# Wider vector operations, a stepped product and one PSUM pool in a fused SSM-convolution and GLU kernel

## The chip, the cores and the metric

The kernel runs on one core of a Trainium2 chip. The metric is the device time of one execution in microseconds. Before the change it is 245.11 us (median of 3 runs, 244.93 to 247.17). The engines of the core are PE (matrix products; PEld is its weight load), DVE (vector), ACT (scalar), POOL and SP, which issues most of the transfers.

## The reference

S = 2048 positions, D = 640 channels, F = 1728; everything is bfloat16.

```python
xn = layernorm(A_q)                                  # over the 640 channels
# A: a short shift filter, a product, and a long convolution over the sequence
k_shift[s] = sum over m of k[s - m] * shift_k[:, m]  # 4 taps
kv = k_shift * v
y = irfft(rfft(kv, 2*S) * rfft(ssm_k, 2*S))[:S]      # long convolution
y = xn * (y + kv * ssm_D)
# B: gated linear unit
h = sigmoid(xn @ w_gate) * (xn @ w_up)
out = A_q + y + h @ w_down
```

## The kernel before, in words

**The GLU.** The sequence is cut into four stretches `tr` of 512 positions. For each, `rec_norm` normalises and `rec_tp` transposes (on PE for 0 and 1, by a transfer through DRAM for 2 and 3), and `rec_fc` makes 14 blocks `fc` of 128 hidden channels: gate and up, five matmuls of 128x512 each (L761), into PSUM tiles of the kind `g` (one bank). ACT takes the sigmoid (L726) and DVE multiplies (L729, L732), with an eviction `ev_u` for the up half where it is in `UP`. `rec_down` makes, for each of the 16 rows `m` of 128 positions, two halves of 320 channels with 14 matmuls each (L775), each half in a `g` bank of its own and added to `acc` by DVE (`fin`, L781). `store` writes `acc` out.

**The convolution.** The FFT is written as matrix products. The channels lie as 4 groups of 160 on the partitions; they are worked off in two halves of five sub-blocks each, `idx` 0 to 9. Each sub-block has 16 channels per group, as two lots `b` of `JS` = 8: channel j and channel j+40. Its steps:
- `rec_kv` (DVE): four multiplications of k with a tap (L474, L475) and three additions (L479), 1024 elements per partition each, and the product with v (L492), which reads both its inputs with a step and writes `kvt` densely. The temporaries lie in `ta`, `tb` and `kvt`.
- `rec_st1` (PE, L512, 32-row blocks), evicted into T; `rec_st2` (PE, L532, 64-row blocks), evicted into S.
- `rec_prod` (DVE): the complex product. Q = X times the other half of H, in the tile P (one buffer, `P2`); X = X times H (L564); then the difference (L568) and the sum (L570) of the two partition halves. Each is done for `b` = 0 and 1 apart, 1024 wide. For the sub-blocks in `SWAP` (3 to 9) two transfers on SP's queue (L551) first bring H's other half into P, and Q is one 128-partition operation for each `b` (L555); for 0 to 2 Q takes two 64-partition operations for each `b` (L561).
- `rec_st3` (PE, L583), evicted into V (in VX).

After the last sub-block `rec_st4` makes six units `u` of up to three rows (L614), evicts them (`ev_y`), multiplies by xn (L621) and adds to `acc` (L622).

**The order.** Every instruction group is recorded by `plan.op`, which numbers it. `ORDER` lists all numbers in the order in which they are emitted, and each engine and each queue runs its own in that order. Most evictions, and the norms of the later rows, can run on ACT or DVE: those whose number is in `ON_DVE` run on DVE. Stores go to ACT's queue, or to SP's if listed.

**The buffers.** `emit` gives each tile a buffer of its kind from `SLOTS`. In PSUM there are three `c` tiles of two banks and two `g` tiles of one bank, apart from each other. `load_h` (L448) brings the convolution filter in with 8 transfers for each part, and `hD` (L452) adds D to its first element, with a step. `load_shift` spreads the taps with two matmuls (csh, L395).

Of the kernel before, what the change touches and what calls it, by code (L numbers as in the profile page):

```python
# [42 lines left out]
def _dft_tables():  # L43
# [82 lines left out]
]  # L126
ON_DVE = [
    52, 106, 108, 110, 142, 148, 150, 506, 514, 534, 562, 574, 646, 831, 883, 917, 922, 970, 971, 972, 973, 975, 976,
    978, 979, 981, 982, 983, 984, 990, 993, 994, 998, 999
# [7 lines left out]
class _Plan:  # L137
# [54 lines left out]
    def emit(self, order, make):  # L192
# [4 lines left out]
        occupant["VB"][0] = "early"  # L197
        where = {}
        for n, o in enumerate(order):
            assert o.deps - {o.seq} <= done  # L200
            mine = []
            for b, tag in o.alloc:
                if b in where:
                    continue
                free = [i for i, c in enumerate(occupant[tag]) if (c is None or left[c] == 0) and (tag, i) not in mine]
                i = min(free, key=lambda i: (occupant[tag][i] is not None, last.get(occupant[tag][i], 0), i))
                mine.append((tag, i))
                occupant[tag][i] = b
# [12 lines left out]
def kernel(  # L221
# [65 lines left out]

    xnd = dr.tile([NQ * P, DM], BF16, name="xnd")
# [3 lines left out]
             "ta": 1, "tb": 1, "T": 2, "S": 2, "P2": 1, "VA": 1, "VB": 1, "c": 3, "g": 2}  # L292
# [3 lines left out]
        "ht0": ([P, 16, 2, N2], BF16), "ht1": ([P, 24, 2, N2], BF16), "kvt": ([P, 2, N2, JS], BF16),  # L296
        "ta": ([P, N2, 2, JS], BF16), "tb": ([P, N2, 2, JS], BF16), "T": ([P, 2 * K1, 2, JS, G], BF16), "S": ([P, 2, 2, JS, G * K1], BF16),
        "P2": ([P, 2, JS, G * K1], BF16),
        "c": ([P, 2, 512], F32), "g": ([P, 512], F32),
# [5 lines left out]
    def make(b, tag, i):  # L305
# [8 lines left out]
        if tag == "VB":  # L314
            return V2[:, 1]
        shape, dt = SHAPE[tag]
        if b.startswith("pst"):
            shape, dt = [P, NC, P], BF16
# [5 lines left out]
        pool = ps if tag in ("c", "g") else wk  # L324
        return pool.tile(shape, dt, name=f"{tag}{i}", tag=f"{tag}{i}")
# [24 lines left out]

    SWAP = (3, 4, 5, 6, 7, 8, 9)
    UP = {(tr, fc) for tr in range(1, 4) for fc in range(12)}
    ZC = (0, 1, 2, 3, 4, 5, 6, 7, 8, 9)
    KT = (0, 1, 2, 3, 4, 5, 6, 7, 8, 9)
    TD = 1
    ACT_STAT = (1, 3)
# [546 lines left out]
```

## Time and profile before

| | before |
|---|---|
| median of 3 runs | 245.11 us |
| profiled execution | 245.07 us |
| its span, first to last instruction | 243.3 us |
| PE busy | 234.2 us (96%), 3700 matmuls |
| PEld busy | 139.4 us (57%) |
| DVE busy | 199.1 us (82%), 335 instructions |
| ACT busy | 186.2 us (77%), 277 instructions |
| granted TensorE clock | 1.0 throughout |

Busy times are of the profiled execution. An operation's mean is its own length; DVE's operations can overlap by some 0.1 us, so means times counts come to more than the busy time. PE's matmuls are pipelined and their ends are modelled, so the time between the starts of two matmuls says more than the length of one.

### The profile page before, as it was taken

The page shows a single profiled execution, that of the slowest core. Times are in us where ns is not written, and L with a number is a line of the kernel's source. Part 1 is how long each engine was busy: PE and PEld are TensorE (multiplying, and loading weights), DVE is VectorE, ACT ScalarE, POOL GpSimd, SP SyncE. Part 2 cuts the span into 40 slices and gives each one's busy share as a digit, 9 for nine tenths or more (in the row PEclk, how much of TensorE's full clock was granted, in tenths as well). Part 3 has the DMA queues.
Part 4 walks back from the last instruction along what each step waited for, and adds up shares of the span by engine and source line. Part 5 has one row for each costly group of instructions (what it writes and reads, how often), then busy time and mean ns, then how long its engine had stood idle before and what let it go on. Part 6 is the DMA issues. An engine that isn't in the chain of part 4 may idle for free.

```text
span 243.3 us, 8435 instructions
## 1 busy us (share of the span) xinstructions
PE 234.2 (96%) x3700; PEld 139.4 (57%) x3700; DVE 199.1 (82%) x335; ACT 186.2 (77%) x277; POOL 0.7 (0%) x6
## 2 busy tenths in 40 slices
PE   8899999999999999999989999998999999999994
PEld 2645445775446546666645555566776565456762
DVE  3623436499899999999999999999989994898973
ACT  5566756978999999796889999986887787656510
POOL 1000000000000000000000000000000000000000
PEclk9999999999999999999999999999999999999999
DMA  6999999998999595199949498593432286972383
GB/s 158 308 224 287 223 328 158 128 167 118 193 197 180 164 288 122 25 140 152 153 88 204 116 218 234 115 203 91 135 87 46 44 268 188 349 253 50 78 236 86
DMA packets 89372, 41.38 MB, mean 170 GB/s; under 512 B 66800, under 2 KB 86072, under 8 KB 89144
## 3 DMA queue, kind: packets, MB, share of 16 engines
q1 hardware_dynamic: 88424, 39.45, 74.5%
q10 hardware_dynamic: 912, 1.39, 2.1%
q8 instruction: 29, 0.48, 0.9%
q14 instruction: 7, 0.06, 0.1%
HBM read 30.61 MB, written 5.24 MB: 147 GB/s over the span
## 4 chain that ended last, share of the span: by engine, by line
PE 76%; DVE 13%; DMA 5%; ACT 2%; issue 2%; SPq 1%; DVEq 0%
PE g L761 40%; PE g L775 21%; PE c L532 7%; DMA w<-in_B_w_up_dram 4%; PE c L583 3%; DVE P L561 2%; PE c L512 2%; PE c L614 2%; DVE kvt L492 2%; DVE ta L479 2%; DVE acc L781 1%; ACT S L338 1%; DVE S L568 1%; DVE S L570 1%; DMA acc<-in_A_q_dram 1%
## 5 line engine op out<-in xcount | busy, mean ns | idle before, releaser
L761 PE MATMUL g<-xnT,w 128*128 128x512 bf16 x340 | 79.9, 379 | 0.6 <-DMA w<-in_B_w_up_dram 0.4
L775 PE MATMUL g<-wd,hT 128*128 128x320 bf16 x448 | 65.9, 299 | 0.7 <-DVE acc L781 0.7
L775 PEld LDWEIGHTS <-hT 128*128 128x128 bf16 x448 | 42.4, 98 | 18.0 <-issue 1.2
L761 PEld LDWEIGHTS <-w 128*128 128x128 bf16 x340 | 31.3, 98 | 34.6 <-DMA w<-in_B_w_up_dram 0.9
L338 ACT CAST S<-c 128x1024 bf16<-128x1024 f32 (+1 forms) x44 | 43.3, 1024 | 5.2 <-PE c L614 3.1
L726 ACT ACTIVATE sig<-g 128x512 bf16<-128x512 f32 x50 | 30.0, 606 | 14.8 <-PE g L761 13.7
L761 PE MATMUL g<-xnT,VX 128*128 128x512 bf16 x180 | 41.4, 379 | 0.0
L761 PEld LDWEIGHTS <-VX 128*128 128x128 bf16 x180 | 16.9, 98 | 19.3
L532 PEld LDWEIGHTS <-Mt 64*128 64x128 f16 x1280 | 19.9, 95 | 8.2 <-issue 7.5
L532 PE MATMUL c<-T,Mt 64*128 64x64 bf16 x1280 | 22.5, 190 | 1.8 <-issue 1.8
L732 DVE TENSOR_TENSOR hT<-sig,g 128x512 bf16<-128x512 bf16 x14 | 9.6, 688 | 17.6 <-PE g L761 17.6
L341 ACT ACTIVATE T<-c 128x1024 bf16<-128x1024 f32 x20 | 20.2, 1031 | 3.9 <-PE c L512 3.9
L338 ACT CAST hT<-g 128x512 bf16<-128x512 f32 x32 | 18.8, 595 | 4.9 <-PE g L761 4.5
L338 ACT CAST T<-c 128x1024 bf16<-128x1024 f32 (+1 forms) x20 | 19.9, 1015 | 2.4 <-PE c L614 1.2
L492 DVE TENSOR_TENSOR kvt<-ta,vt 128x1024 bf16<-128x1024 bf16 x10 | 21.5, 2148 | 0.1
L338 ACT CAST VX<-c 128x1024 bf16<-128x1024 f32 x18 | 17.8, 1021 | 4.5 <-PE c L583 4.0
L781 DVE TENSOR_TENSOR acc<-g,acc 128x320 bf16<-128x320 f32 x32 | 15.5, 488 | 6.0 <-PE g L775 5.6
L729 DVE TENSOR_TENSOR hT<-sig,hT 128x512 bf16<-128x512 bf16 x36 | 14.8, 421 | 3.7 <-ACT sig L726 3.0
L568 DVE TENSOR_TENSOR S<-S 64x1024 bf16<-64x1024 bf16 x20 | 13.7, 686 | 0.7
L570 DVE TENSOR_TENSOR S<-P 64x1024 bf16<-64x1024 bf16 x20 | 13.8, 689 | 0.5
L479 DVE TENSOR_TENSOR ta<-ta,tb 128x1024 bf16<-128x1024 bf16 x20 | 13.8, 690 | 0.2
L474 DVE TENSOR_TENSOR tb<-kt,sT 128x1024 bf16<-128x1024 bf16 x20 | 13.8, 688 | 0.2
(83 smaller groups left out, 217.1 us busy)
## 6 DMA issues: line engine op xcount, KB each, us to landing
w<-in_B_w_up_dram SPq DMA_DIRECT2D x7, 640.0 KB, 5.9
w<-in_B_w_gate_dram SPq DMA_DIRECT2D x6, 640.0 KB, 5.4
P<-S SPq DMA_DIRECT2D x14, 256.0 KB, 3.7
kt<-in_A_k_dram SPq DMA_DIRECT2D x8, 320.0 KB, 7.4
vt<-in_A_v_dram SPq DMA_DIRECT2D x8, 320.0 KB, 6.0
xnd<-VX SPq DMA_DIRECT2D x4, 640.0 KB, 6.5
acc<-in_A_q_dram SPq DMA_DIRECT2D x12, 160.0 KB, 7.7
ht<-in_A_ssm_k_dram SPq DMA_DIRECT2D x16, 96.0 KB, 3.5
```

The lines of the kernel that those rows point to most:

```text
L338: fa = lambda: nc.scalar.copy(out=out_fn(), in_=in_fn())
L341: fa = lambda: nc.scalar.activation(out_fn(), in_fn(), ACT.Copy, scale=scale)
L479: dve("tt2", 1024, lambda: nc.vector.tensor_tensor(tl[a][:], tl[a][:], tl[c][:] if c != o else tl[c].rearrange("p b n j -> p n b j"), ALU. ...
L492: dve("ttkt" if kt else "tt2", 1024, lambda: nc.vector.tensor_tensor(by_j(tl[o]) if kt else tl[o][:], tl[a].rearrange(form), sl(tl[vb], 0) ...
L532: nc.tensor.matmul(tl[c][:, b, 64 * kk:64 * kk + 64], lhsT=Mb[rows, k, 64 - 64 * r:192 - 64 * r], rhs=tl[T][rows, 2 * k + r].rearrange("p ...
L568: dve("tt2", 1024, lambda b=b: nc.vector.tensor_tensor(X(b)[0:64], X(b)[0:64], X(b)[64:P], ALU.subtract), r=[(S_, "p", b)], w=[(S_, "z", b)])
L570: dve("tt2", 1024, lambda b=b: nc.vector.tensor_tensor(X(b)[64:P], Q(b)[0:64], Q(b)[64:P], ALU.add), r=[(S_, "z", b), (Z, b, 0)], w=[(S_, ...
L726: act("sig", 512, lambda: nc.scalar.activation(tl[sg][:], pv(0), ACT.Sigmoid), r=[pk(0)], w=[(sg,)], alloc=[(sg, "sig")])
L729: dve("gmul2", 512, lambda: nc.vector.tensor_tensor(hT[:, fc, :], tl[sg][:], hT[:, fc, :], ALU.mult), r=[(sg,), (hk, fc, 0)], w=[(hk, fc)])
L761: nc.tensor.matmul(tl[c][:], lhsT=w()[:, k, o:o + P], rhs=tl[X][:, k, :], start=(k == 0), stop=(k == NC - 1))
L775: nc.tensor.matmul(tl[p_][:, 0:320], lhsT=hT[:, fc, t4 * P:(t4 + 1) * P], rhs=wd[:, fc, 320 * i:320 * i + 320], start=(fc == 0), stop=(fc ...
L781: dve("fin", 320, lambda i=i, m=m, pd=pd: nc.vector.tensor_tensor(acc[:, m, 320 * i:320 * i + 320], tl[pd[i]][:, 0:320], acc[:, m, 320 * i ...
```

## The change

- The two lots of a sub-block are now neighbouring channels 2j and 2j+1, so that its 16 channels lie side by side. `rec_kv` makes the taps as two multiplications 2048 wide (two taps at once, through an access pattern whose rows overlap), one addition 2048 wide and one 1024 wide. The second multiplication's tile lies in `P2`, the buffer of P; `tb` is gone.
- The product with v reads its inputs in runs of 16 and writes `kvt` with a step of 64 elements; only sub-block 0 (`ROWS`) reads with a step and writes densely.
- `rec_prod` makes each step of the complex product for both `b` in one operation 2048 wide.
- V is evicted into every second element.
- The filter comes in with 4 transfers for each part instead of 8; the taps are spread by 8 narrower matmuls instead of 2.
- PSUM is one tile of eight banks. A `c` tile takes an even pair whose two banks are free, a `g` tile any free bank, first one whose neighbour is taken.
- Both halves of a down row share a pair of banks and are added by one DVE operation 640 wide, except for row 15 (`FIN2`).
- `ORDER` and `ON_DVE` are new. More norms and evictions are on DVE: norms 4 to 13 and 15, where it had been 4, 9 and 11, and 20 evictions instead of 14. The last down rows are 12 and 13 instead of 14 and 15; the last store is that of rows 12 and 13.

```diff
@@ emit
+                if tag in ("c", "g"):
+                    age = [-1 if x is None else n if left[x] else last[x] for x in banks]
+                    ok = [age[i] < n and ("g", i) not in mine for i in range(8)]
+                    if tag == "c":
+                        i = min((i for i in range(4) if ok[2 * i] and ok[2 * i + 1]),
+                                key=lambda i: (max(age[2 * i], age[2 * i + 1]), i))
+                        take = (2 * i, 2 * i + 1)
+                    else:
+                        i = min((i for i in range(8) if ok[i]), key=lambda i: (ok[i ^ 1], age[i], i))
+                        take = (i,)
...
+    psa = ps.tile([P, 8, 512], F32, name="psa")
...
-             "ta": 1, "tb": 1, "T": 2, "S": 2, "P2": 1, "VA": 1, "VB": 1, "c": 3, "g": 2}
+             "ta": 1, "T": 2, "S": 2, "P2": 1, "VA": 1, "VB": 1, "c": 4, "g": 8}
...
@@ load_shift
-                nc.tensor.matmul(tl[c][:, i, 0:2 * CG], lhsT=FRb[:, 128:256], rhs=sr()[:, 2 * CG * i:2 * CG * i + 2 * CG],
-                                 start=True, stop=True)
+                x = sr()[:, 2 * CG * i:2 * CG * i + 2 * CG].rearrange("p (d m) -> p m d", m=4)
+                for m in range(4):
+                    nc.tensor.matmul(tl[c][:, i, HALF * m:HALF * m + HALF], lhsT=FRb[:, 128:256], rhs=x[:, 3 - m],
+                                     start=True, stop=True)
@@ rec_kv
-        mul(a, 0, "ta")
-        mul(t1, 1, "tb")
-        mul(o, 2, "kvt")
-        add(t1)
-        mul(t2, 3, "tb")
-        add(o)
-        add(t2)
-        kt = idx in KT
-        form = "p n b j -> p j b n" if kt else "p n b j -> p b n j"
-        dve("ttkt" if kt else "tt2", 1024, lambda: nc.vector.tensor_tensor(by_j(tl[o]) if kt else tl[o][:], tl[a].rearrange(form),
-                                                                  sl(tl[vb], 0).rearrange(form), ALU.mult),
+        def mul(t, r):
+            k = lambda: tl[kb][:, r:r + N2, j0:j0 + 2 * JS]
+            s = sT[:, r:r + 2, half * HALF + j0:half * HALF + j0 + 2 * JS].unsqueeze(2)
+            dve("tap", 2048, lambda: nc.vector.tensor_tensor(
+                tl[t][:], bass.AP(k().tensor, k().offset, [k().ap[0], [HALF, 2], [HALF, N2], [1, 2 * JS]]),
+                s.to_broadcast((P, 2, N2, 2 * JS)), ALU.mult), r=kr + [("s",)], w=[(t,)], alloc=[(t, "ta" if t == a else "P2")])
+        mul(a, 2)
+        mul(b, 0)
+        dve("tap", 2048, lambda: nc.vector.tensor_tensor(tl[a][:], tl[a][:], tl[b][:], ALU.add), r=[(b,)], w=[(a,)])
+        dve("tt2", 1024, lambda: nc.vector.tensor_tensor(tl[a][:, 0], tl[a][:, 0], tl[a][:, 1], ALU.add), w=[(a,)])
+        rows = idx in ROWS
+        f = (lambda t: t.rearrange("p n (j b) -> p j b n", b=2)) if rows else (lambda t: t.rearrange("p n (j b) -> p n j b", b=2))
+        out = lambda: tl[o][:] if rows else tl[o].rearrange("p j b n -> p n j b")
+        dve("ttkt", 1024, lambda: nc.vector.tensor_tensor(out(), f(tl[a][:, 0]), f(tl[vb][:, :, j0:j0 + 2 * JS]), ALU.mult),
+            r=[(a,)] + vr_, w=[(o,)], alloc=[(o, "kvt")])
@@ rec_prod (the sub-blocks with a swap)
-            for b in range(2):
-                dve("tt2", 1024, lambda b=b: nc.vector.tensor_tensor(Q(b), X(b), Q(b), ALU.mult),
-                    r=[(Z, "h", 0), (Z, "h", 1)], w=[(Z, b, 0)])
+            dve("pr", 2048, lambda: tt(Q(), X(), Q(), ALU.mult), r=[(Z, "h", 0), (Z, "h", 1)], w=[(Z, 0), (Z, 1)])
...
+        dve("pr", 2048, lambda: tt(X(), X(), H(), ALU.mult), r=[(Z, 0), (Z, 1)] + sr, w=[(S_, "p")])
+        dve("pr", 2048, lambda: tt(X()[0:64], X()[0:64], X()[64:P], ALU.subtract), r=[(S_, "p")], w=[(S_, "z")])
+        dve("pr", 2048, lambda: tt(X()[64:P], Q()[0:64], Q()[64:P], ALU.add), r=[(S_, "z"), (Z, 0), (Z, 1)], w=[(S_, "q")])
@@ rec_st3
-            co = b * JH + sub * JS
-            ev("ev_V", 1024, lambda co=co: tl[V].rearrange("p n r d -> p (n r) d")[:, :, co:co + JS],
+            co = 2 * sub * JS + b
+            ev("ev_V", 1024, lambda co=co: tl[V].rearrange("p n r d -> p (n r) d")[:, :, co:co + 2 * JS - 1:2],
@@ rec_down
-            for i in range(2):
-                dve("fin", 320, lambda i=i, m=m, pd=pd: nc.vector.tensor_tensor(
-                    acc[:, m, 320 * i:320 * i + 320], tl[pd[i]][:, 0:320], acc[:, m, 320 * i:320 * i + 320], ALU.add),
+            for i0, i1 in (((0, 1), (1, 2)) if m in FIN2 else ((0, 2),)):
+                dve("fin", 320 * (i1 - i0), lambda i0=i0, i1=i1, m=m, p_=p_: nc.vector.tensor_tensor(
+                    acc[:, m, 320 * i0:320 * i1].rearrange("p (a d) -> p a d", d=320), tl[p_][:, i0:i1, 0:320],
+                    acc[:, m, 320 * i0:320 * i1].rearrange("p (a d) -> p a d", d=320), ALU.add),
```

More of the change, by code (lines that the diff above doesn't have):

```diff
@@ L197, in emit @@
         occupant["VB"][0] = "early"
+        banks = [None] * 8
         where = {}
@@ L204, in emit @@
                     continue
[L205 to L208, printed above, removed]
+                if tag in ("c", "g"):
[8 more added lines that the diff above has]
+                        take = (i,)
+                    for k in take:
+                        banks[k] = b
+                        mine.append(("g", k))
+                else:
+                    free = [i for i, c in enumerate(occupant[tag]) if (c is None or left[c] == 0) and (tag, i) not in mine]
+                    i = min(free, key=lambda i: (occupant[tag][i] is not None, last.get(occupant[tag][i], 0), i))
+                    mine.append((tag, i))
+                    occupant[tag][i] = b
                 where[b] = i
@@ L295 @@
         "kt": ([P, N2 + 3, HALF], BF16), "vt": ([P, N2, HALF], BF16),
-        "ht0": ([P, 16, 2, N2], BF16), "ht1": ([P, 24, 2, N2], BF16), "kvt": ([P, 2, N2, JS], BF16),
-        "ta": ([P, N2, 2, JS], BF16), "tb": ([P, N2, 2, JS], BF16), "T": ([P, 2 * K1, 2, JS, G], BF16), "S": ([P, 2, 2, JS, G * K1], BF16),
+        "ht0": ([P, 16, 2, N2], BF16), "ht1": ([P, 24, 2, N2], BF16), "kvt": ([P, JS, 2, N2], BF16),
+        "ta": ([P, 2, N2, 2 * JS], BF16), "T": ([P, 2 * K1, 2, JS, G], BF16), "S": ([P, 2, 2, JS, G * K1], BF16),
         "P2": ([P, 2, JS, G * K1], BF16),
-        "c": ([P, 2, 512], F32), "g": ([P, 512], F32),
     }
@@ L315, in make @@
             return V2[:, 1]
+        if tag == "c":
+            return psa[:, 2 * i:2 * i + 2]
+        if tag == "g":
+            if b.startswith("pst"):
+                return psh[:, i, 0:NC * P].rearrange("p (c t) -> p c t", c=NC)
+            return psa[:, i]
         shape, dt = SHAPE[tag]
-        if b.startswith("pst"):
-            shape, dt = [P, NC, P], BF16
+        if b.startswith("kb"):
+            shape = SHAPE["ta"][0]
         if b == "Bt":
@@ L323, in make @@
             shape, dt = [P, 2, n * DM], BF16
-        pool = ps if tag in ("c", "g") else wk
-        return pool.tile(shape, dt, name=f"{tag}{i}", tag=f"{tag}{i}")
+        return wk.tile(shape, dt, name=f"{tag}{i}", tag=f"{tag}{i}")
     def pe(kind, n, fn, **kw):
@@ L444, in load_h @@
         b = f"ht{half}{part}"
+        hc = lambda: tl[b].rearrange("p j b n -> p (j b) n")
         for g in range(G):
-            for p in range(2):
-                c0 = (half * G + g) * HALF + p * JH
-                dma(lambda e, g=g, p=p, c0=c0: e.dma_start(tl[b][g * N1:(g + 1) * N1, :, p, :], h3[:, c0 + j0:c0 + j1, :]), 32 * (j1 - j0), 128,
-                    w=[(b, g, p)], alloc=[(b, f"ht{part}")] if g + p == 0 else ())
-        d0 = half * HALF
-        dv = Dt[:, d0:d0 + HALF].rearrange("p (b j) -> p j b", b=2)[:, j0:j1, :]
-        dve("hD", 2 * (j1 - j0), lambda: nc.vector.tensor_tensor(tl[b][:, :, :, 0], tl[b][:, :, :, 0], dv, ALU.add),
-            r=[("D",), ("D0",)], w=[(b, g, p) for g in range(G) for p in range(2)])
-    def by_j(t):
-        return t.rearrange("p b n j -> p (b n j)").rearrange("p (j b n) -> p j b n", j=JS, b=2)
+            c0 = (half * G + g) * HALF
+            dma(lambda e, g=g, c0=c0: e.dma_start(hc()[g * N1:(g + 1) * N1], h3[:, c0 + 2 * j0:c0 + 2 * j1, :]), 64 * (j1 - j0), 128,
+                w=[(b, g)], alloc=[(b, f"ht{part}")] if g == 0 else ())
+        dv = Dt[:, half * HALF + 2 * j0:half * HALF + 2 * j1]
+        dve("hD", 2 * (j1 - j0), lambda: nc.vector.tensor_tensor(hc()[:, :, 0], hc()[:, :, 0], dv, ALU.add),
+            r=[("D",), ("D0",)], w=[(b, g) for g in range(G)])
     def rec_kv(idx):
@@ L460, in rec_kv @@
         kb, vb = f"kt{half}", f"vt{half}"
-        j0 = sub * JS
-        a, o = f"ka{idx}", f"kvt{idx}"
+        j0 = 2 * sub * JS
+        a, b, o = f"ka{idx}", f"kb{idx}", f"kvt{idx}"
         kr = [(kb, "h")] + [(kb, g) for g in range(G)]
         vr_ = [(vb, g) for g in range(G)]
-        def sl(t, r0):
-            return t[:, r0:r0 + N2, :].rearrange("p n (b j) -> p n b j", b=2)[:, :, :, j0:j0 + JS]
-        def sh(m):
-            s = sT[:, m:m + 1, half * HALF:(half + 1) * HALF].rearrange("p o (b j) -> p o b j", b=2)
-            return s[:, :, :, j0:j0 + JS].to_broadcast((P, N2, 2, JS))
@@ L501, in rec_st1 @@
         hj = j0 - HPART[part][0]
-        src = [(f"kvt{idx}",)] if x == 0 else [(hb, g, p) for g in range(G) for p in range(2)]
+        src = [(f"kvt{idx}",)] if x == 0 else [(hb, g) for g in range(G)]
         T = f"T{idx}"
@@ L509, in f @@
                     rows = slice(N1 * g, N1 * g + N1)
-                    st = (tl[hb][rows, hj + j, :, :] if x else by_j(tl[f"kvt{idx}"])[rows, j] if idx in KT
-                          else tl[f"kvt{idx}"][rows, :, :, j])
+                    st = tl[hb][rows, hj + j] if x else tl[f"kvt{idx}"][rows, j]
                     nc.tensor.matmul(tl[cs[g // 2]][:, g % 2, 64 * j:64 * j + 64], lhsT=st.rearrange("p b n -> p (b n)"),
                                      rhs=Fb[rows, 0:64], start=True, stop=True, tile_position=(N1 * g, 0))
-        pe("st1s" if x == 0 and idx not in KT else "st1", 32, f, r=src + [("A",)] + ([] if first else [(T, "a")]),
+        pe("st1", 32, f, r=src + [("A",)] + ([] if first else [(T, "a")]),
            w=[(c,) for c in cs] + ([(T, "a")] if first else []), alloc=[(c, "c") for c in cs] + ([(T, "T")] if first else []))
@@ L577, in rec_st3, with f @@
             c = f"c3_{idx}_{b}"
-            zc = idx in ZC
-            def f(b=b, c=c, zc=zc):
+            def f(b=b, c=c):
                 for j in range(JS):
-                    o = tl[c][:, j // 4, 128 * (j % 4):128 * (j % 4) + 128]
-                    nc.tensor.matmul(o, lhsT=tl[S_][:, b, 0, j, :], rhs=Ab[:, 2 if zc else 0, :], start=True, stop=zc)
-                    if not zc:
-                        nc.tensor.matmul(o, lhsT=tl[Z][:, b, j, :], rhs=Ab[:, 1, :], start=False, stop=True)
+                    nc.tensor.matmul(tl[c][:, j // 4, 128 * (j % 4):128 * (j % 4) + 128], lhsT=tl[S_][:, b, 0, j, :],
+                                     rhs=Ab[:, 2, :], start=True, stop=True)
             z = (sub, b) == (0, 0)
-            pe("st3" if zc else "st3d", 8 * (2 - zc), f, r=([(S_, "z", b), (S_, "q", b)] if zc else [(Z, b, 0), (S_, "p", b)]) + [("A",)] + ([] if z else [(V, "a")]),
+            pe("st3", 8, f, r=[(S_, "z"), (S_, "q"), ("A",)] + ([] if z else [(V, "a")]),
                w=[(c,)] + ([(V, "a")] if z else []), alloc=[(c, "c")] + ([(V, "VA" if half == 0 else "VB")] if z else []))
-            co = b * JH + sub * JS
-            ev("ev_V", 1024, lambda co=co: tl[V].rearrange("p n r d -> p (n r) d")[:, :, co:co + JS],
+            co = 2 * sub * JS + b
+            ev("ev_V", 1024, lambda co=co: tl[V].rearrange("p n r d -> p (n r) d")[:, :, co:co + 2 * JS - 1:2],
                lambda c=c: tl[c].rearrange("p a n -> p (a n)").rearrange("p (j n) -> p n j", j=JS),
@@ L769, in rec_down, with f @@
             m = 4 * tr + t4
-            pd = [f"pd{m}_{i}" for i in range(2)]
+            p_ = f"pd{m}"
             for i in range(2):
                 for c0, c1 in ((0, 7), (7, 14)):
-                    def f(c0=c0, c1=c1, t4=t4, p_=pd[i], i=i):
+                    def f(c0=c0, c1=c1, t4=t4, p_=p_, i=i):
                         for fc in range(c0, c1):
-                            nc.tensor.matmul(tl[p_][:, 0:320], lhsT=hT[:, fc, t4 * P:(t4 + 1) * P],
+                            nc.tensor.matmul(tl[p_][:, i, 0:320], lhsT=hT[:, fc, t4 * P:(t4 + 1) * P],
                                              rhs=wd[:, fc, 320 * i:320 * i + 320],
@@ L778, in rec_down @@
                     pe("down", c1 - c0, f, r=[("hT", fc) for fc in range(c0, c1)] + [("wd", fc) for fc in range(c0, c1)] +
-                       ([("z",)] if c1 == 14 else []), w=[(pd[i],)], alloc=[(pd[i], "g")] if c0 == 0 else ())
-            for i in range(2):
-                dve("fin", 320, lambda i=i, m=m, pd=pd: nc.vector.tensor_tensor(
-                    acc[:, m, 320 * i:320 * i + 320], tl[pd[i]][:, 0:320], acc[:, m, 320 * i:320 * i + 320], ALU.add),
-                    r=[(pd[i],)], w=[("fin", m, i)], c=[("acc", m, q) for q in range(4)])
+                       ([("z",)] if c1 == 14 else []), w=[(p_, i)], alloc=[(p_, "c")] if c0 == i == 0 else ())
+            for i0, i1 in (((0, 1), (1, 2)) if m in FIN2 else ((0, 2),)):
+                dve("fin", 320 * (i1 - i0), lambda i0=i0, i1=i1, m=m, p_=p_: nc.vector.tensor_tensor(
+                    acc[:, m, 320 * i0:320 * i1].rearrange("p (a d) -> p a d", d=320), tl[p_][:, i0:i1, 0:320],
+                    acc[:, m, 320 * i0:320 * i1].rearrange("p (a d) -> p a d", d=320), ALU.add),
+                    r=[(p_, i) for i in range(i0, i1)], w=[("fin", m, i) for i in range(i0, i1)], c=[("acc", m, q) for q in range(4)])
     make_identity(nc, ident)
```

47 lines of the change are left out of this document (15 added, 32 removed), and 85 rows, old and new, of the table ORDER.

## The prediction

> **What bounds the kernel now.** I read the table by stretches first, then the chain that ended last, then the waits of TensorE. The columns of the first are: stretch, length, busy PE, PEld, DVE, ACT, POOL with counts, clock, DMA share, GB/s.
>
> ```profile
> 60.00:80.00 20.00, 20.00 (x391) 10.38 (x390) 18.91 (x39) 19.31 (x29) 0.00 (x0) 1.00 0.96 185
> 100.00:120.00 20.00, 19.54 (x369) 12.95 (x367) 19.44 (x30) 16.24 (x20) 0.00 (x0) 1.00 0.90 124
> 160.00:180.00 20.00, 18.93 (x427) 13.61 (x420) 19.21 (x29) 16.20 (x18) 0.00 (x0) 1.00 0.44 105
> 200.00:220.00 20.00, 20.00 (x275) 10.44 (x268) 15.24 (x25) 13.14 (x19) 0.00 (x0) 1.00 0.79 250
> ```
>
> From 60 to 205 us PE and DVE are both about 97% busy, so neither can be slowed for nothing. Busy PE is modelled, so I take its pitch from blocks of the chain (start, length, what):
>
> ```profile
> 138.92 2.16 PE g L761 x10
> 149.46 3.34 PE g L761 x15
> 163.80 1.07 issue
> 166.57 1.90 PE g L775 x14
> 131.53 1.51 PE c L532 x96
> 239.75 0.49 DVE acc L781
> ```
>
> A gate/up matmul has a pitch of 0.216 us, a down matmul 0.1357, a st2 matmul 0.0157. With 0.0106 (st1), 0.056 (st3, first, tp) and 0.0099 (st4) from blocks read likewise, the counts give 520x0.216 + 448x0.1357 + 1280x0.0157 + 640x0.0106 + 280x0.056 + 512x0.0099 = 220.8 us of PE work. The first real matmul starts at 8.54 us and the last ends at 239.75: 231.2 us. Of the 10.4 us between, about 40 x 0.11 = 4.4 go when a full-height block gives way to a 32- or 64-row block (2.27 instead of 2.16). The waits of PE hold the rest:
>
> ```profile
> PE c L532 <- issue: 1.8, 2, 1.1
> PE g L775 <- DVE acc L781: 0.7, 2, 0.4
> PE g L761 <- DMA w<-in_B_w_up_dram: 0.4, 1, 0.4
> PE g L761 <- DVE acc L781: 0.2, 1, 0.2
> ```
>
> So PE is the bound. Other engines hold it for 1.3 us past the start, and 1.85 are "issue", for which nothing here is responsible. **There is little to win, and DVE, its equal in load, can lose.**
>
> **DVE operations.** The rows (form, count, busy, mean ns of one):
>
> ```profile
> L492 DVE TENSOR_TENSOR kvt<-ta,vt 128x1024 bf16<-128x1024 bf16 x10 | 21.5, 2148 | 0.1
> L474 DVE TENSOR_TENSOR tb<-kt,sT 128x1024 bf16<-128x1024 bf16 x20 | 13.8, 688 | 0.2
> L621 DVE TENSOR_TENSOR S<-S 128x1920 bf16<-128x1920 bf16 x2 | 2.3, 1152 | 0.0
> L452 DVE TENSOR_TENSOR ht<-ht,Dt 128x48 bf16<-128x48 bf16 x2 | 0.7, 370 | 0.0
> L452 DVE TENSOR_TENSOR ht<-ht,Dt 128x32 bf16<-128x32 bf16 x2 | 0.6, 298 | 0.2 <-DMA At<-dftA 0.2
> ```
>
> (1152-688)/896 = 0.518 ns per element and 158 ns fixed, so 2048 wide takes 1.22 us. The taps keep their elements (7x1024 per sub-block before, 3x2048+1024 after) and shed 3 instructions in each of 10. Products shed 4 in the 7 sub-blocks with a swap and 5 in the other 3: 43. Down sums shed 15. That is 88. In DVE's timeline an operation starts 0.60 us after one it does not depend on and 0.72 after one that it does; 0.53 of that are elements. Each merged instruction so saves 0.07 to 0.19; I take 0.12, as both kinds are mixed: 88x0.12 = 10.6 us, 8.8 of it (73) between 60 and 205. The new runs are 16 elements long where L474 has 8, and that row is already at the paired rate. If the overlapping rows lost it, 2048 would take 158+2x1061 = 2.28 us, 21 us more over 20 taps; the nearest row says no.
>
> The new list gives DVE work of ACT. Between 60 and 205: five more norms (437 ns each on DVE) and one T and one S eviction (1.22): 4.6 us. Elsewhere: three norms at 40 to 60, two y and two u evictions after 205, where the stretches show DVE with time to spare. ACT is relieved of about 8x0.92 + 2x1.03 + 2x0.96 + 2x0.60 = 12.5 us. Net for DVE in the saturated stage: -8.8+4.6 = -4.2 us, **if the V-product costs what it did**.
>
> **The V-product** is the unknown: nine of ten now read runs of 16 and write one 2-byte element every 128 bytes. No row has just that. Below: an unpaired pass, as in the 1.22 us evictions of 1024 from PSUM. Above: hD (L452), which steps 128 bytes on read and write: (370-298)/16 = 4.5 ns per element, so 0.16+4.6 = 4.77 us. Nearest is L492 itself, where both reads step by 32 and 160 bytes and the write does not: 1.94 ns per element. One stepped side then, one now; half of hD's 4.5 is 2.25, or 2.46 us, close by. I take 2.15, no change, and keep 1.22 to 4.77.
>
> [...]
>
> V evictions now write every second element, on ACT 18 times. The nearest rows, T evictions that write pairs with gaps (1.02 to 1.03 us), say no change; twice that would add 18 us to ACT, of which 12.5 are free.
>
> **PE and its banks.** csh becomes 8 matmuls at a pitch of 0.056 instead of 0.27 us for two: +0.2. One pool of eight banks and one pair per down row let a down block start without the bank just being added: the 0.7+0.2 us of waits on L781 go. At the start four gate blocks use the first whole gate tile before an up tile is needed (before: two, with 0.36 of waiting). The up tile comes two x loads of 160 KB later, 1.3 us at 241 GB/s, against 2.2 us of blocks: -0.36. Sixteen fewer SP issues of h lie beside other work, bytes unchanged.
>
> **The end.** Before, the last down block is followed by a 320-wide add and a 20 KB store. The new order ends with rows 12 and 13, one 640-wide add (0.16+640x1.04 ns = 0.82, so +0.33) and four stores of 80 KB:
>
> ```profile
> out_dram<-acc SPq DMA_DIRECT2D x4, 20.0 KB, 1.5
> out_dram<-acc ACTq DMA_DIRECT2D x3, 80.0 KB, 3.0
> ```
>
> 1.5 us more to land, in a busier moment; the 246 KB more at 240 GB/s would be 1.0. I take 1.0 (bounds 0.6 to 1.5). Nothing hides it.
>
> **Sum**, from the profiled execution (span 243.3, total 245.07, median of runs 245.11): +0.2 csh, +0.33 and +1.0 at the end, -0.9 banks, -0.36 start = +0.3, so **245.4 us**.
>
> **Rivals.**
> *Slower: the stepped write makes DVE the bound*, in kv1 to kv9, 60 to 205 us. The st3 blocks already wait on the last product now and then (PEld <- S L570, 0.7 us), so there is nearly no reserve: it decides from 2.15+4.2/9 = 2.6 us. At 3.2 us: 9x1.05-4.2 = 5.3, 250.7; at hD's rate 9x2.62-4.2 = 19 us, 264. For: hD. Against: L492 had two streams stepped and paid only 1.94. Chance 0.18; most of it near the lower price.
>
> *Slower: the tap's second tile now shares P2 with the products.* A swap into P2 must await the tap's add and the preceding product. From the freeing operation to the later landing the swap needs about 0.1+0.68+4.0 = 4.8 us:
>
> ```profile
> L551 SPq DMA_DIRECT2D P<-S x14: 595/602/1282, 124.0 to 204.0; - x14
> DMA to landing us min/median/max: 3.3/3.7/4.1
> ```
>
> In the new order DVE has 4.9 to 6.4 us of other work in that time for sub-blocks 3 to 8, but only 0.69+0.69+0.69 = 2.1 for the ninth. Queued behind this wait are the ninth product, st3 and, through V, all of st4. DVE stands 2.7 us there. If no reserve remains, PE waits with it, and 0.3 us at each other swap: 245.4+2.7+6x0.3 = 249.9. For: the trace already has 0.7 us of this wait. Against: st3_9 lies six gate/up blocks (6.5 us) behind st3_8. Decides if DVE has won less than about 3 us by then. Chance 0.14.
>
> *Faster: the V-product at 1.22 us.* DVE wins 9x0.93+4.2 = 12.6 us and no longer holds PE. Then 8.54 + 220.8+0.2 + 4.4 + 1.85 = 235.8 for PE's end; the end part of 243.3-239.75 = 3.55 grows by 1.33, and 1.77 lie outside the span: 242.4 us. For: both reads become contiguous, and an eviction whose output has gaps, T's on DVE, still takes 1.22. Against: both stepped rows. Chance 0.20.
>
> **Numbers.** Forecast 0.48, its own range 243.5 to 247.5 (end 0.6 to 1.5, waits won between none and 2.6, V-product up to 2.7). One per cent, about what a measurement of this kernel can tell from no change, is 2.45 us. Faster 0.20 and slower 0.32 are the rivals. For 8 in 10 the range runs from 242.2 to 250.7: it leaves out the dear half of the first rival and a little at both ends.
>
> **What would show it.** L492's successor at 2.1 to 2.5 us for nine and 2.15 for one; 2048-wide rows at 1.22; DVE busy near 199.1-10.6+9.6 = 198, ACT near 174; PE's last block within 1.5 us of 239.75; about 4.9 us from there to the end instead of 3.55; a DVE wait on P<-S near the ninth product. A V-product above 2.6, long waits of st3 on DVE, or a PE end before 237 would make it wrong.

## The result and the profile after

The changed kernel is slower: 270.63 us (median, 269.36 to 270.82) against 246.14 for the kernel before in the same runs, a ratio of 1.0985, 95% interval 1.0908 to 1.1062. The forecast was 245.4 us, with a range from 242.2 to 250.7. The profiled execution took 270.68 us, with a span of 268.9, 25.6 us longer than before.

The profile page of the changed kernel, its busy times and three of its rows of 40 slices:

```profile
PE 240.5 (89%) x3706; PEld 142.0 (53%) x3706; DVE 220.1 (82%) x261; ACT 178.3 (66%) x263; POOL 0.7 (0%) x6
...
PE   8799999999897599996995969959979799999993
...
DVE  3404545899999999999999899699899986888891
...
PEclk9999999999997999999997997989999999999999
```

The same rows before:

```profile
PE   8899999999999999999989999998999999999994
DVE  3623436499899999999999999999989994898973
PEclk9999999999999999999999999999999999999999
```

Before, PE and DVE stood at 9 together through most of the middle. Now PE has many gaps and DVE few. DVE's busy time rose by 21 us, though it has 74 instructions fewer. The clock row, 9 throughout before, has dips to 7. The same stretches as in the prediction (stretch, length, busy PE, PEld, DVE, ACT, POOL with counts, clock, DMA share, GB/s):

```profile
60.00:80.00 20.00, 18.74 (x296) 9.38 (x295) 19.87 (x17) 15.42 (x22) 0.00 (x0) 1.00 1.16 190
100.00:120.00 20.00, 19.90 (x467) 14.10 (x466) 19.44 (x20) 19.58 (x22) 0.00 (x0) 1.00 0.75 146
160.00:180.00 20.00, 16.15 (x275) 7.98 (x276) 17.75 (x19) 14.75 (x21) 0.00 (x0) 0.90 0.53 153
200.00:220.00 20.00, 18.02 (x407) 12.06 (x398) 18.06 (x17) 11.42 (x13) 0.00 (x0) 1.00 0.43 120
```

At 160 to 180 us PE was busy for 16.15 us, where it had been for 18.93, and its clock stood at 0.90 on average. The costliest groups (form, count, busy, mean ns of one, idle time before them):

```profile
L496 DVE TENSOR_TENSOR kvt<-ta,vt 128x1024 bf16<-128x1024 bf16 x10 | 44.9, 4489 | 0.1
L356 ACT CAST VX<-psa 128x1024 bf16<-128x1024 f32 x18 | 22.4, 1279 | 4.3 <-PE psa L575 4.2
L486 DVE TENSOR_TENSOR ta<-kt,sT 128x2048 bf16<-128x2048 bf16 x10 | 12.2, 1222 | 0.6 <-ACT kt L356 0.5
L563 DVE TENSOR_TENSOR S<-S 128x2048 bf16<-128x2048 bf16 x10 | 12.2, 1222 | 0.2
```

The operations 2048 wide take 1.22 us, as predicted. The product with v does not take what was predicted: the one that reads with a step takes 2151 ns, and the nine that write with a step stand near 4.74 us (the median of all ten is 4743 ns). And who waits (us in total, times, longest):

```profile
PEld L514 <- DVE kvt L496: 9.1, 4, 3.6
PE psa L514 <- DVE kvt L496: 7.5, 4, 3.1
PE psa L752 <- ACT sig L717: 5.6, 2, 3.0
ACT sig L717 <- DVE hT L720: 10.0, 6, 3.4
```

The waits of PEld and PE lie over each other and are not to be added. Before, the list of waits has none of PE or PEld for a product with v, and sig waited 0.5 us for L729, L720's counterpart:

```profile
ACT sig L726 <- DVE hT L729: 0.5, 1, 0.5
```

The chain that ended last is the work followed back from the last instruction, at each step to what released it. Two places of it (start, length, what):

```profile
139.28 4.67 DVE kvt L496
144.00 0.41 PE psa L514 x32
144.41 5.03 PE psa L752 x15
...
156.19 4.77 DVE kvt L496
161.00 0.41 PE psa L514 x32
161.42 5.03 PE psa L752 x15
```

Here the chain runs through a long product on DVE and goes over to PE at st1 of its sub-block. The 15 gate/up matmuls behind it take 5.03 us; a group of 15 took 3.34 before. The granted clock was 0.50 for a part of them (146 to 148 and 163 to 165 us). PE had waited 3.12 and 2.12 us ahead of these two st1 blocks.

### The profile page after: what moved, and what is told of

It is laid out like the page before. It is cut to its first block, busy times and chain, and to the rows that moved or that the text cites. A ratio compares the mean times of both kernels' runs of the same rounds, so it can differ in the third digit from the quotient of the medians.

```text
span 268.9 us, 8321 instructions
## 1 busy us (share of the span) xinstructions
PE 240.5 (89%) x3706; PEld 142.0 (53%) x3706; DVE 220.1 (82%) x261; ACT 178.3 (66%) x263; POOL 0.7 (0%) x6
## 4 chain that ended last, share of the span: by engine, by line
DVE 41%; PE 33%; DMA 15%; SPq 5%; issue 4%; ACT 1%; DVEq 0%
DVE kvt L496 16%; PE psa L752 16%; PE psa L766 9%; DMA acc<-in_A_q_dram 4%; DMA wd<-in_B_w_down_dram 3%; DMA VX<-in_B_w_up_dram 3%; SPq L446 3%; DMA kt<-in_A_k_dram 3%; PE psa L534 3%; DVE ta L491 3%; DVE acc L772 2%; DVE S L564 2%; DVE P L486 2%; DVE ta L486 2%; PE psa L605 2%
## 5 line engine op out<-in xcount | busy, mean ns | idle before, releaser
L752 PE MATMUL psa<-xnT,w 128*128 128x512 bf16 x340 | 83.7, 395 | 6.1 <-DVE hT L714 2.8
L766 PE MATMUL psa<-wd,hT 128*128 128x320 bf16 x448 | 67.4, 299 | 0.1
L717 ACT ACTIVATE sig<-psa 128x512 bf16<-128x512 f32 x52 | 30.7, 608 | 29.0 <-PE psa L752 11.3
L752 PE MATMUL psa<-xnT,VX 128*128 128x512 bf16 x180 | 42.3, 381 | 3.0 <-ACT sig L717 3.0
L496 DVE TENSOR_TENSOR kvt<-ta,vt 128x1024 bf16<-128x1024 bf16 x10 | 44.9, 4489 | 0.1
L356 ACT CAST S<-psa 128x1024 bf16<-128x1024 f32 (+1 forms) x42 | 40.4, 1020 | 4.8 <-PE psa L534 2.5
L356 ACT CAST T<-psa 128x1024 bf16<-128x1024 f32 (+1 forms) x19 | 18.8, 1037 | 10.5 <-PE psa L514 10.5
L356 ACT CAST VX<-psa 128x1024 bf16<-128x1024 f32 x18 | 22.4, 1279 | 4.3 <-PE psa L575 4.2
L534 PE MATMUL psa<-T,Mt 64*128 64x64 bf16 x1280 | 22.6, 194 | 0.1
L359 ACT ACTIVATE T<-psa 128x1024 bf16<-128x1024 f32 x20 | 19.9, 1043 | 3.0 <-PE psa L514 2.9
L720 DVE TENSOR_TENSOR hT<-sig,hT 128x512 bf16<-128x512 bf16 x36 | 15.0, 430 | 4.0 <-ACT sig L717 3.6
```

Of the source, the lines that this page charges most:

```text
L356: fa = lambda: nc.scalar.copy(out=out_fn(), in_=in_fn())
L359: fa = lambda: nc.scalar.activation(out_fn(), in_fn(), ACT.Copy, scale=scale)
L496: dve("ttkt", 1024, lambda: nc.vector.tensor_tensor(out(), f(tl[a][:, 0]), f(tl[vb][:, :, j0:j0 + 2 * JS]), ALU.mult), r=[(a,)] + vr_, w=[ ...
L534: nc.tensor.matmul(tl[c][:, b, 64 * kk:64 * kk + 64], lhsT=Mb[rows, k, 64 - 64 * r:192 - 64 * r], rhs=tl[T][rows, 2 * k + r].rearrange("p ...
L717: act("sig", 512, lambda: nc.scalar.activation(tl[sg][:], pv(0), ACT.Sigmoid), r=[pk(0)], w=[(sg,)], alloc=[(sg, "sig")])
L720: dve("gmul2", 512, lambda: nc.vector.tensor_tensor(hT[:, fc, :], tl[sg][:], hT[:, fc, :], ALU.mult), r=[(sg,), (hk, fc, 0)], w=[(hk, fc)])
```

## The experiments

**The stepped write taken away, all else kept (e1_rows_all).**

```diff
-    ROWS = (0,)
+    ROWS = (0, 1, 2, 3, 4, 5, 6, 7, 8, 9)
```

> The changed kernel with all ten V-products in the reading form (ROWS = 0 to 9), nothing else. Theory A (the stepped write is the cause: nine products at 4.75 us where 2.15 were expected put 23.4 us on DVE while it is the bound): the product falls to 2.15 us, DVE busy to about 220-23 = 197 us, the granted clock returns to 1.0, the time to 244 to 248 us. Theory B (the new order, the coarser products and the tile shared in P2 are the cause, the product lies mostly beside other work): the time stays above 256 us.

246.48 us against 246.57: ratio 0.9998 (0.9947 to 1.0049), span 243.3, clock 1.0. Its product group and its waits:

```profile
L496 DVE TENSOR_TENSOR kvt<-ta,vt 128x1024 bf16<-128x1024 bf16 x10 | 21.6, 2158 | 0.1
```
```profile
DVE P L557 <- DMA P<-S: 3.8, 3, 2.5
PEld L514 <- DVE kvt L496: 1.4, 2, 1.0
```

One line of the change holds the whole loss. The rest together is worth nothing that can be measured, which fits the sum of the prediction (+0.3 us). DVE waits 3.8 us for the swap in the shared `P2`, and the time is still that of the kernel before.

**The stepped write alone, put into the kernel before (e2_step_alone).**

```diff
-        form = "p n b j -> p j b n" if kt else "p n b j -> p b n j"
+        form = "p n b j -> p j b n" if idx == 0 else "p n b j -> p n b j"
+        back = "p j b n -> p j b n" if idx == 0 else "p j b n -> p n b j"
...
-        ... by_j(tl[o]) if kt else tl[o][:], tl[a].rearrange(form),
+        ... by_j(tl[o]).rearrange(back), tl[a].rearrange(form),
```

> The kernel before with nine of its ten V-products written with a step of 128 bytes and read in runs of 8, in its own order and with its own taps, products and PSUM pools. Theory A: each of the nine goes from 2.15 to about 4.75 us, DVE was 97% busy in that stage, so nearly all of 23 us shows: 262 to 270 us. Theory B: less than half of it shows, under 256 us.

266.71 us, ratio 1.0806 (1.0710 to 1.0902), that is some 20 us. `kvt` took 43.9 us in ten operations instead of 21.5. So 22.4 us of DVE work cost 20 us of time, with none of the other edits. The mean clock was 1.0 in the profiled execution and 0.981 to 0.987 in the other three.

**What makes the operation dear (micro_steps).** The operations alone, three of each, 1024 elements per partition, in a program that does nothing else (shown without its loops; notes to the reader behind #):

```diff
+        tt(pit(64), aj, aj, ALU.mult)                                    # L128: all dense
+        tt(pit(64).rearrange("p j n -> p n j"), an, vn, ALU.mult)        # L130: write every 128 bytes
+        tt(pit(72).rearrange("p j n -> p n j"), an, vn, ALU.mult)        # L138: write every 144 bytes
+        tt(of.rearrange("p (j n) -> p n j", j=16)[:], an, vn, ALU.mult)  # L146: float32 written every 256 bytes
+        tt(an, pit(64).rearrange("p j n -> p n j"), vn, ALU.mult)        # L160: read every 128 bytes
+        tt(blk(2)[0], blk(2)[1], blk(2)[2], ALU.mult)                    # L162: pairs of neighbours written
...
+        nc.scalar.copy(out=V[:, :, 0:57:8], in_=src)                     # L173: ACT, write every 16 bytes
```

> Leaves out the whole computation (the output is zero): one DVE or ACT operation of 1024 elements after another, three of each form. If the price is that of a 128-byte step (accesses that fall on the same part of the memory), a pitch of 65, 66, 68 or 72 elements instead of 64 falls to 1.2 to 2 us and 128 elements stays at 4.7. If it is that of writing single 2-byte elements far apart, every pitch costs about 4.7 and a 4-byte output at the same element step is cheap. If reading and writing are alike, a read stepped by 128 bytes costs about as much as the write. Blocks of 2, 4 and 8 neighbouring elements on the write side fall in proportion to the number of runs.

```profile
L130 DVE TENSOR_TENSOR o<-a,v 128x1024 bf16<-128x1024 bf16 x3 | 14.3, 4755 | 0.1
...
L173 ACT CAST V<-pt 128x1024 bf16<-128x1024 f32 x3 | 14.0, 4681 | 0.1
...
L138 DVE TENSOR_TENSOR o<-a,v 128x1024 bf16<-128x1024 bf16 x3 | 13.7, 4574 | 0.1
...
L146 DVE TENSOR_TENSOR of<-a,v 128x1024 f32<-128x1024 bf16 x3 | 5.9, 1963 | 0.1
...
L160 DVE TENSOR_TENSOR a<-o,v 128x1024 bf16<-128x1024 bf16 x3 | 5.6, 1878 | 0.1
...
L162 DVE TENSOR_TENSOR o<-a,v 128x1024 bf16<-128x1024 bf16 x3 | 3.7, 1226 | 0.1
```

The dense form took 686 ns (L128). Lone 2-byte elements, whose neighbours in memory are not written with them, took 4.6 to 4.8 us for 1024 at pitches of 128 to 144 and of 256 bytes alike, 4.43 at 160 and 5.27 at 192: none of these pitches escapes it, so it is not a collision at one pitch. Reading with a step of 128 bytes took 1.88 us; a float32 output, written every 256 bytes, 1.96; pairs of neighbours, 1.23. Longer blocks were expected to fall further and did not: blocks of 4 and 8 took 1.93 and 2.15 us. Their reads are as stepped as those of the pairs, and why pairs are cheaper was not settled. ACT took 4.68 us when it wrote every eighth element, 16 bytes apart, but only 1.27 for every second element, against 1.01 dense. What makes the product dear is **the write of lone 2-byte elements** far apart (4.43 to 5.27 us at 128 bytes and more), not steps as such.

**V written densely (e3_rows_dense_v)**, on top of e1; the channels within each 16 then stand in another order, and that of the output with them.

```diff
-            co = 2 * sub * JS + b
-            ... [:, :, co:co + 2 * JS - 1:2],
+            co = 2 * sub * JS + b * JS
+            ... [:, :, co:co + JS],
```

> As the first (all V-products in the reading form), and V is evicted into 8 neighbouring elements instead of every second one. The channels of each 16 then stand in another order in the output: this shows the cost of the eviction alone. If the 0.26 us more of each of 18 ACT evictions (1.28 instead of 1.02) matters, 4.6 us of ACT time go and the time falls by 1 us or more against the first; if ACT has room, it stays within 0.5 us of it.

245.23 us, ratio 0.9976 (0.9934 to 1.0018). The eviction takes 1018 ns instead of 1285. The median is 1.25 us under e1's, the ratio 0.002 under, and the two intervals overlap: no difference can be told, and a gain of about 1 us is not ruled out. So most of ACT's extra 18 x 0.26 = 4.7 us was hidden, if not all.

**The product in pairs (e4_pairs).** The innermost loop runs over two neighbouring positions, so that each write is an aligned 4 bytes, in all ten sub-blocks:

```diff
-        f = (lambda t: t.rearrange("p n (j b) -> p j b n", b=2)) if rows else (lambda t: t.rearrange("p n (j b) -> p n j b", b=2))
-        out = lambda: tl[o][:] if rows else tl[o].rearrange("p j b n -> p n j b")
+        f = lambda t: t.rearrange("p (c i) k -> p c k i", i=2)
+        out = lambda: tl[o].rearrange("p j b (c i) -> p c (j b) i", i=2)
```

> The changed kernel with all ten V-products written in pairs: the loop goes over n in steps of two, the 16 channels, and the two n inside, so that each write is two neighbouring elements. In the single measurement that form took 1.23 us, against 4.75 stepped and 2.15 reading. DVE busy falls to about 197.4-9.3 = 188 us. If PE alone is the bound of the version with reading products (my account of the kernel before), the time falls by no more than 1%, ratio 0.99 to 1.00 to the kernel before. If DVE still held it there, the 9 us show: ratio 0.97 or less.

```profile
L495 DVE TENSOR_TENSOR kvt<-ta,vt 128x1024 bf16<-128x1024 bf16 x10 | 12.2, 1220 | 0.1
```

242.46 us against 245.88: ratio 0.9867 (0.9817 to 0.9917), DVE busy 188.8 us. That lies between the two expectations: a little more than the 1% of a bound by PE alone, and far less than the 9 us that DVE sheds against e1. In the profiled execution PE makes up 94% of the chain that ended last. The prediction's faster rival, a product of 1.22 us, had PE's floor at 242.4; the six runs lie between 241.1 and 244.5.

**The same pairs in the kernel before (e5_before_pairs)**, as two operations of 512, one for each b.

```diff
+            for x in range(2):
+                nc.vector.tensor_tensor(by_j(tl[o])[:, :, x].rearrange("p j (c i) -> p c j i", i=2),
+                                        tl[a][:, :, x].rearrange("p (c i) j -> p c j i", i=2),
+                                        sl(tl[vb], 0)[:, :, x].rearrange("p (c i) j -> p c j i", i=2), ALU.mult)
```

> The kernel before with its ten V-products written in pairs, as two operations of 512 elements (0.69 us each, 1.38 for 2.15), nothing else. DVE sheds 7.7 us. PE-bound: ratio 0.99 to 1.00. DVE also the bound: ratio 0.975 or less.

245.32 us, ratio 0.9956 (0.9922 to 0.9990), DVE busy 191.5 us: 7.6 us less of DVE are worth about 1 us, as for a kernel bound by PE. With a cheap product, the rest of the change (with one operation instead of two for the product) is thus worth 0.9867/0.9956 = 0.991, about 0.9%; the two intervals do not overlap. With the reading product of 2.15 us nothing of it could be measured (e1).

**Pairs and a dense V (e6_pairs_dense_v)**, on top of e4, with st3's matmuls regrouped so that the order of the channels stays.

```diff
-                for j in range(JS):
-                    nc.tensor.matmul(tl[c][:, j // 4, 128 * (j % 4):128 * (j % 4) + 128], lhsT=tl[S_][:, b, 0, j, :],
+                for l in range(2):
+                    for j in range(4):
+                        nc.tensor.matmul(tl[c][:, l, 128 * j:128 * j + 128], lhsT=tl[S_][:, l, 0, 4 * b + j, :],
...
-            ... [:, :, co:co + 2 * JS - 1:2],
+            ... [:, :, co:co + JS].rearrange("p x (j l) -> p x j l", l=2),
```

> As e4, and the st3 blocks are regrouped so that one block holds four j of both lots: V is then evicted into 8 neighbouring elements, with the output's channels in their right order. ACT evictions of V fall from 1.28 to 1.02 us. If the version is bound by PE, no change against e4 (within 0.3%); the earlier pair of runs hinted at 0.2%.

242.23 us, ratio 0.9850 (0.9815 to 0.9886), the best version here, not told apart from e4. V's evictions took 1023 ns.

**The end (e8_pairs_end)**: e6 with row 13 in two halves like row 15, and rows 12 and 13 stored apart.

```diff
-    FIN2 = (15,)
+    FIN2 = (13, 15)
...
-    store(12, 14)
+    store(12, 13)
+    store(13, 14)
```

> As e6, and the end is cut finer: row 13 is added in two halves and rows 12 and 13 are stored apart, so that after the last matmul a 320-wide add and four stores of 40 KB are left instead of 640 and 80 KB. By my account of the end, 0.33 us for the add and 0.5 to 0.8 us for the store: ratio 0.003 to 0.005 below e6. If the landing time does not depend on the size, only 0.33 us.

243.06 us, ratio 0.9884 (0.9849 to 0.9919): no gain. The stretch from PE's last matmul (236.72) to the end (241.4) was 4.7 us, with a 320-wide add and small stores, where e6 had 4.4 (236.44 to 240.8). So a smaller last store did not shorten the end; what sets its length stays open.

**How much DVE can bear: two stepped (f1_two_stepped) and five (f2_five_stepped).**

```diff
-    ROWS = (0,)
+    ROWS = (0, 1, 2, 4, 5, 7, 8, 9)
```
```diff
-    ROWS = (0,)
+    ROWS = (0, 2, 4, 6, 8)
```

> The changed kernel with only two V-products stepped (sub-blocks 3 and 6), the other eight reading. DVE bears 2 x 2.6 = 5.2 us more than with none. If the reserve of 4.2 us that the prediction counted on is real, at most 1 us of it shows (ratio to the kernel before 1.00 to 1.005). If there is none, all of it: ratio 1.02.

> Five V-products stepped (1, 3, 5, 7, 9): 13 us more on DVE. With a reserve of 4.2 us: 9 us, ratio 1.036. Without: 13 us, ratio 1.053. If the whole 24 us of nine come at a constant rate of 2.7 each, also 1.054; if the last 4 to 6 of the 24 come from the halved TensorE clock after long waits, the clock is still 1.0 here and each costs 2.2 or less: 1.045 or less.

Two: 253.52 us, ratio 1.0328 (1.0282 to 1.0374), 8.0 us for 2 x 2.6 = 5.2 us of DVE work. Five: 260.01 us, 1.0591 (1.0539 to 1.0642), 14.5 us for 13.0. So 0, 2, 5 and 9 stepped products cost 0, 8.0, 14.5 and 24.2 us by the ratios: there is no part that comes free, and the price of one falls from 4.0 to 2.7 us. The forecast that the clock would still be 1.0 with five missed: it was 0.979 to 0.987, and with two 0.980 to 0.989. The timeline of f1 around the first of the two shows what is behind (start, length; in brackets the wait before it):

```profile
81.46 4.75 DVE L496 TENSOR_TENSOR kvt<-ta,vt 128x1024 bf16<-128x1024 bf16 x1
...
86.63 0.42 DVE L720 TENSOR_TENSOR hT<-sig,hT 128x512 bf16<-128x512 bf16 x1
87.14 0.60 ACT L717 ACTIVATE sig<-psa 128x512 bf16<-128x512 f32 x1 [3.45 <-DVE hT L720]
87.79 4.44 PE L752 MATMUL psa<-xnT,VX 128*128 128x512 bf16 x12 [3.40 <-ACT sig L717]
```

A gate product of 0.42 us (L720) stands behind the long product in DVE's order. It reads the `sig` tile that ACT's next sigmoid wants; the sigmoid frees the bank that PE's next gate block wants. So ACT stops for 3.45 and PE for 3.40 us at a place that has nothing to do with `kvt`. In e1, with a product of 2.15 us, the same place has waits of 1.07 and 1.03 us: 2.6 us more on DVE are 2.4 us more here. The 15 matmuls then take 5.08 us instead of 3.34, and at the second place, behind a wait of 2.57 us that e1 does not have, 5.03. Both groups stand in the chain that ended last:

```profile
87.79 5.08 PE psa L752 x15
...
151.98 5.03 PE psa L752 x15
```

The waits added (2.4 and 2.6 us) and the two slowed groups (1.7 us each) come to 8.4 us, which accounts for the 8.0 measured: here the lowered clock (0.91 on average at 80 to 100 and at 140 to 160 us, 1.00 in the stretches between) reached the end.

**PE kept at work through the waits (f3_kept_warm).** On top of the changed kernel, 14 and 9 matmuls of 128x512 with no use ahead of st1 of sub-blocks 5 and 6:

```diff
+            for _ in range({5: 14, 6: 9}.get(idx, 0) if x == 0 else 0):
+                nc.tensor.matmul(tl[cs[0]][:, 0], lhsT=Ab[:, 0, :], rhs=wd[:, 0, 0:512], start=True, stop=True)
```

> The changed kernel as it is (nine stepped), with 14 and 9 matmuls of 128x512 that no one reads put in front of the two st1 blocks of sub-blocks 5 and 6, where TensorE waited 3.1 and 2.1 us for the product and then ran 15 gate and up matmuls at half the granted clock (5.03 us instead of 3.34). If the wait is what lowers the clock, these stay at full clock: 1.7 us less for each, the time 2 to 4 us under that of the changed kernel though TensorE has more work. If the clock falls for another reason, nothing is won, and up to 1 us lost.

The timeline of f3 at those two places:

```profile
141.94 3.19 PE L511 MATMUL psa<-wd,At 128*128 128x512 bf16 x14
...
145.58 3.41 PE L754 MATMUL psa<-xnT,w 128*128 128x512 bf16 x15
...
158.27 2.10 PE L511 MATMUL psa<-wd,At 128*128 128x512 bf16 x9
...
161.37 3.41 PE L754 MATMUL psa<-xnT,w 128*128 128x512 bf16 x15
```

The gate/up groups of 15 took 3.41 us each where this view has 5.10 for the changed kernel: with the wait filled, the groups at these two places were not slowed. But the time was 269.25 us, ratio 1.0977 (1.0925 to 1.1030), against 1.0985 (1.0908 to 1.1062) without them. One reason stands in the same trace: at 92 us, where nothing was filled in, a group of 15 behind a wait of 3.09 us took 5.08 us, and in the changed kernel's trace the same group is not slowed:

```profile
92.13 3.40 PE L752 MATMUL psa<-xnT,VX 128*128 128x512 bf16 x15 [3.01 <-ACT sig L717]
```

So 1.7 of the 3.4 us were lost again, and the mean clock hardly rose (0.979 to 0.987 over four executions, against 0.973 to 0.981). The runs do not show what the lowered clock costs the changed kernel.

**Where the price begins (micro_runs).** All inputs dense, only the write changes, again 1024 elements (shown without its loops; notes to the reader behind #):

```diff
+        tt(lone(2), a[:], a[:], ALU.mult)        # L144: 2 bytes every 4
+        tt(lone(4), a[:], a[:], ALU.mult)        # L148: 2 bytes every 8
+        tt(lone(8), a[:], a[:], ALU.mult)        # L152: 2 bytes every 16
+        tt(runs(2, 8), a[:], a[:], ALU.mult)     # L156: 4 bytes every 16
+        tt(runs(2, 8, 1), a[:], a[:], ALU.mult)  # L158: 4 bytes every 16, from an odd element
```

> Leaves out the whole computation (the output is zero): DVE products of 1024 elements, both inputs dense, the output in runs of one, two or four 2-byte elements at several steps, and single 4-byte elements. If a single 2-byte element that is written alone in its 8 bytes is what costs, steps of 4 and 6 bytes are cheap and from 8 bytes on the price is about 4.6 us; runs of two cost 1.23 at every step, also from an odd start. [...]

```profile
L152 DVE TENSOR_TENSOR w<-a 128x1024 bf16<-128x1024 bf16 x3 | 14.1, 4688 | 0.1
...
L148 DVE TENSOR_TENSOR w<-a 128x1024 bf16<-128x1024 bf16 x3 | 7.3, 2429 | 0.1
L158 DVE TENSOR_TENSOR w<-a 128x1024 bf16<-128x1024 bf16 x3 | 7.3, 2425 | 0.1
...
L144 DVE TENSOR_TENSOR w<-a 128x1024 bf16<-128x1024 bf16 x3 | 3.9, 1299 | 0.1
...
L156 DVE TENSOR_TENSOR w<-a 128x1024 bf16<-128x1024 bf16 x3 | 3.2, 1066 | 0.1
```

The price of lone elements did not jump at one step, it climbed: 1.30, 1.86, 2.43, 2.99 and 4.69 us at 4, 6, 8, 10 and 16 bytes, and at pitches of 128 to 256 bytes it lay between 4.43 and 5.27 (micro_steps). The expectation, with a jump to about 4.6 us at 8 bytes, did not have that. Aligned pairs took 0.69 to 1.08 us, and those every 16 bytes 2.43 when they start on an odd element, where 1.23 was expected.

## Why the prediction was wrong, by its steps

- **The V-product** is the step that failed. It took 2.15 us as "nearest is L492 itself", counted its two stepped reads as one stepped side, and let the stepped write stand in for the other. The runs show that reads and writes are not interchangeable: 1.88 us for a read at 128 bytes, 4.76 for a write. L492, which writes densely, said nothing about a write. hD was the only row with 2-byte elements written apart, and its 4.5 ns per element gave 4.77 us; measured are 4.74. Halving it to 2.25, for one stepped side instead of two, had no ground in a row, and the runs show the other: the read beside the write was free (4723 ns for read and write both stepped in place, 4755 for the write alone). The range let the product go up to 2.7 us: no run shows that term; the nine stepped products took about 4.74.
- **The slower rival** (DVE becomes the bound) is what happened, at its upper price. It said 264 us; measured are 270.6. The product's own excess was right: 9 x 2.59 = 23.3 us, against 24.2 by the ratio. What failed is the **-4.2 us of DVE** that it set against it. Between 60 and 205 us e1 has 1.9 us less of DVE than the kernel before (136.2 against 138.2) and is no faster, and in f1 two stepped products cost their whole extra length in waits (5.0 of 5.2 us), and 3.4 us by the clock besides. Nor did the idle time there help: DVE was busy for 95% of that stage before the change and PE for 98%, where the prediction has 97% for both. A reserve spread over many instructions is not there at the one place where an instruction is 2.6 us longer. "Decides from 2.6 us" falls with it. Its chance of 0.18, most near the lower price, was too low, as the one row with such a write gave the dear price.
- **What else the stalls cost.** The prediction has no term for PE's clock. Behind some of the waits it fell: PE is busy 240.5 us in the changed kernel and 233.3 in e1. In f1 that loss, 2 x 1.7 us, reached the end; in the changed kernel it stays open, as f3 won it back at two places and lost half of it at a third. In the changed kernel it was 0.50 at 146 to 148 and 163 to 165 us, behind waits of 3.12 and 2.12 us ahead of st1. Other waits as long left it up: 3.01 us in the changed kernel (1.00 at 92 to 94 us), 2.88 in f2 (the next 15 matmuls took 3.41 us), 3.2 in e2's profiled execution (mean clock 1.0). Why these differ was not settled.
- **DVE's other operations** held. 1.22 us for 2048 wide, with no loss of rate on the overlapping rows of the taps. Without the stepped write, DVE was busy 197.4 us (e1), predicted 198; ACT 177.3, predicted near 174; V's evictions, put at no change, added 4.7.
- **V's evictions** were put at no change and took 1.28 us instead of 1.02. In e3 no difference in time could be told.
- **The second tap's tile in P2**: DVE does wait for the swap, 3.5 us in the changed kernel and 3.8 in e1. The cost of 2.7 us and more did not come: e4, at 242.46, stands on the floor of 242.4 reckoned without this wait, though it still has 4.2 us of it. A version with a buffer of its own was not tried.
- **The end** was put at +1.33 us and is +0.82 (264.53 to 268.9 is 4.37, before 3.55). The 640-wide add takes the predicted 0.82 us, but the stores of 80 KB land in 1.8 to 2.0 us, not 3.0. e8 shows no gain from smaller ones.
- **The start** was to gain 0.36 us. That wait is gone, but the changed kernel and e1 wait some 1.4 us for a transfer of weights, and their first gate matmul starts at 13.02 and 12.88 us instead of 12.66. This and the waits for banks are too small to be told apart in the time.
- **The faster rival** named the price (1.22 us) and the floor (242.4) that pairs reached in e4. To meet the floor within 0.1 us is in part luck, as e4's six runs spread over 3.4 us. Its condition, that a write with gaps costs no more, held for aligned pairs (1.22 us) and not for the lone elements of this change (4.74).

## What to carry to other kernels

Price a stepped access by its operand and element size, and look for a row whose *write* has the same pattern: a row with stepped reads says nothing of it (1024 elements took 1.88 us read and 4.76 written at 128 bytes). If 2-byte elements must be scattered, put two neighbours innermost so that aligned 4 bytes are written: the same product went from 4.74 to 1.22 us and the kernel from 1.0985 to 0.9867 of the time before. Longer blocks of this product were not better (1.93 and 2.15 us). On an engine that is nearly always busy, look at the short operations queued behind a long one and at the buffers that they free, before a saving elsewhere on that engine is set against it.

## What was not expected of the hardware

- Lone 2-byte writes were dear on ACT as on DVE: 4.68 and 4.62 us for 1024 elements from PSUM at 16 bytes apart, 1.27 and 1.26 at 4 bytes apart, 1.01 and 1.22 dense.
- 2-byte elements written apart took more than twice as long as 4-byte ones: 4.69 against 1.96 us for 1024 at 16 bytes, 4.71 against 1.96 at 256 bytes.
- Alignment counted: pairs every 16 bytes took 1.07 us from an even element and 2.43 from an odd one; runs of four every 64 bytes 0.69 and 1.27.
